# Length-39 transforms by sums and differences of q and 39 - q, as 64x64 products in quarters of the array, for the later batches of a fused filter-and-experts kernel

## The chip, the cores and the metric

The kernel runs on one core of a Trainium2 chip. The metric is the device time of one execution in microseconds (us), the median of several runs. A profile of one such execution shows every instruction of the engines: TensorE (PE for its matmuls, PEld for its weight loads), VectorE (DVE), ScalarE (ACT), GpSimd (POOL) and SyncE (SP, which here only issues DMAs). Everything is float32.

## What is computed

Two layers, one after the other, on `x` of 8 batches x 2496 tokens x 256 channels:

```python
X = np.fft.rfft(x, axis=1)                 # along the 2496 tokens
Y = X * (filt_r + 1j * filt_i)[None]
y = np.fft.irfft(Y, n=2496, axis=1)        # then (8*2496, 256)

logits = y @ w_gate                        # 8 experts
e = argmax(logits); gate = softmax(logits)[e]
out = gate * (relu(y @ w1[e]) @ w2[e])     # token by token, 256 -> 1024 -> 256
```

## The kernel before

**The transform.** 2496 = 39 x 64, and 39 and 64 have no common factor, so the long transform is a 39 x 64 transform in two dimensions. A token is named by a pair (q, t), q below 39 and t below 64. For each batch there are four stages on TensorE, each with its own table as the stationary operand:

- stage A (`stage_a`, L336): the real length-39 transform over q. Three values of t lie below each other in the partitions, so a table of 3 x 39 = 117 rows and 3 x 40 = 120 columns (`tas`) turns a tile of 117 partitions into 20 real and 20 imaginary coefficients for three t. A batch has 64 values of t in 22 columns of 256 channels. They come in chunks of four (`CH`: five chunks of four and one of two); a matmul takes two columns, 512 elements, so a full chunk costs two matmuls (L342).
- stage B (L356) and stage C (L382): the length-64 transform and its inverse, 128 x 128 tables; between them DVE multiplies by the filter (L363 to L372).
- stage D (`stage_d`, L391): the inverse length-39 transform, the same shape as A turned round: 120 rows in, 117 rows out (L401; the batch's last two columns L405, one of 120 rows and one of 40).

Between A and B and between C and D the data goes through DRAM (`zd`, `ud`), which turns it: A's result is stored with 120 partitions, B reads 64 and 64. After each matmul of A and D the function `evac` copies the PSUM bank to SBUF on DVE or ACT, whichever its own estimate (`either`) says is free first. Batch 0 takes another way (`first_a` and so on), with no DRAM.

**Routing.** Stage D's result `yo` is transposed on TensorE (`turn_y`, L476), multiplied by the gate's weights (`logits`, L490, four products of 32 columns each next to each other in the array), turned back (L501), and some 20 small DVE operations (`route`) find each token's expert and its place in a list of rows in DRAM. GpSimd then scatters the rows with one indirect DMA for each column (`scatter`, L617): 22 for a batch.

**The experts.** As soon as a batch's rows are listed, tiles of 512, 256 or 128 rows of one expert are loaded (`rows_in`), transposed (L750), multiplied by w1 (L793, seven products in place of eight by sums that GpSimd and DVE form, or L834 without them), then by w2 (L851), scaled by the gate (L856) and scattered to the output by GpSimd (L857).

**The order.** The whole program is one hand-made order: every engine's instructions are issued in the order in which a planner in the kernel's last part emits them. `slot(k)` lists the transform's steps of one round with a place in the round and a price in us of TensorE: in slot k stand stages B and C of batch k, stage A of batch k+1 and stage D and routing of batch k-1. `experts()` yields the experts' pieces, and the main loop mixes the two streams, so that TensorE has expert work between transform steps. An engine takes its instructions strictly in that order: where one waits, all behind it on the same engine wait. `now`, `free` and `lands` are the planner's estimates; nothing measures at run time. `more_loads` issues the loads of x, z and u ahead, through 7 buffers (`NIN`), in the order in which the steps will need them. After about 930 us the transform is over and only experts' work is left.

Of the kernel before, what the change touches and what calls it, by code (L numbers as in the profile page):

```python
# [38 lines left out]

def token(q, t):  # L40
    return (q * N2 * pow(N2, -1, N1) + t * N1 * pow(N1, -1, N2)) % S


def coefficients():

    k = np.arange(S)
    of = np.zeros((N2, N1), int)
    of[k * pow(N1, -1, N2) % N2, k * pow(N2, -1, N1) % N1] = k
    return of[:, :NF]


def dft_tables():
# [27 lines left out]
    for j in range(NB):  # L80
# [6 lines left out]

    return {
# [6 lines left out]
        "valid": valid.reshape(TP, NG),  # L95
    }


def lay_x(x):

    out = np.zeros((x.shape[0], P, NG, D), x.dtype)
    q = np.arange(N1)
    for j in range(NB):
        for i in range(len(range(j, N2, NB))):
            out[:, j * N1:(j + 1) * N1, i] = x[:, token(q, NB * i + j)]
    return out
# [12 lines left out]
def kernel(  # L119
# [13 lines left out]
    valid: bass.AP,  # L133
    out: bass.AP,
# [47 lines left out]
    tas = cst.tile([TP, TK], F32, name="tas")  # L182
    tbs = cst.tile([P, P], F32, name="tbs")
    tcs = cst.tile([P, P], F32, name="tcs")
    tds = cst.tile([TK, TP], F32, name="tds")
# [6 lines left out]
    tri = cst.tile([TP, TP], F32, name="tri")  # L192
    ones = cst.tile([TP, P], F32, name="ones")
    segs = {w: cst.tile([P, E * w], F32, name=f"seg{w}") for w in (8, NG % 8)}
    ids0 = cst.tile([TP, NG], F32, name="ids0")
    vld = cst.tile([TP, NG], F32, name="vld")
# [63 lines left out]
    def load_rest():  # L260
        nc.sync.dma_start(out=tds, in_=td)
        nc.vector.memset(wg, 0.0)
        nc.sync.dma_start(out=wg[:, :, :E], in_=moe_w_gate.rearrange("(i p) e -> p i e", p=P))
        nc.sync.dma_start(out=ids0, in_=ids)
        nc.sync.dma_start(out=vld, in_=valid)

    def make_constants():
# [3 lines left out]
            out=tri, in_=ones[:, :TP], compare_op=ALU.is_gt, fill=0.0, base=0, pattern=[[1, TP]], channel_multiplier=-1  # L271
# [15 lines left out]
    def columns(ap, i0, n):  # L287
# [4 lines left out]
        if m < n:  # L292
            yield NS, slice(m, n), rows[(NG - 1) * TK:, :].rearrange("(i p) d -> p i d", p=NS)

# [29 lines left out]
    def load_z(b, c):  # L324
        f0, n = FH[c]
        zi = fin(("z", b, c))
        nc.sync.dma_start(out=zi[:HP, :n], in_=zd[b][:, f0:f0 + n, :])
        nc.sync.dma_start(out=zi[HP:, :n], in_=zd[b][:, NF + f0:NF + f0 + n, :])

    def load_u(b, c):  # L330
        i0, n = CH[c]
        ui = fin(("u", b, c))
        for r, m, v in columns(ud[b], i0, n):
            nc.sync.dma_start(out=ui[:r, m], in_=v)

    def stage_a(b, c):  # L336
        i0, n = CH[c]
        xt = ins.pop(("x", b, c))
        zo = sb.tile([TK, 4, D], F32, tag="st", name="zo", bufs=4)
        for j in range(0, n, 2):  # L340
            p = bank()
            mm(p[:TK, :], lhsT=tas, rhs=xt[:TP, j:j + 2, :], start=True, stop=True)  # L342
            evac(zo[:, j:j + 2, :], p[:TK, :].rearrange("p (t d) -> p t d", t=2), 512)
# [31 lines left out]
    def stage_c(b, f):  # L375
# [8 lines left out]
        if j == 2:  # L384
            f0 = f - 2
            move(ud[b][:, f0:f0 + 4, :], uo[:HP])
            move(ud[b][:, NF + f0:NF + f0 + 4, :], uo[HP:])
# [3 lines left out]
    def stage_d(b, c):  # L391
        if c == 0:
            lgs[b] = sb.tile([TP, NG, E], F32, tag="lg", name="lg")
# [3 lines left out]
        yo = outs["o", b, c] = sb.tile([P, 4, DR], F32, tag="y", name="yo", bufs=YB)[:TP]  # L397
        for j in range(0, n, 2):
            p = bank()
            if i0 + j + 2 < NG:  # L400
                mm(p[:TP, :], lhsT=tds, rhs=ui[:TK, j:j + 2, :], start=True, stop=True)  # L401
            else:

                for i, k in enumerate((TK, NS)):
                    mm(p[:TP, i * D:(i + 1) * D], lhsT=tds[:k, :], rhs=ui[:k, j + i, :], start=True, stop=True)  # L405
# [6 lines left out]
    def first_a(c):  # L412
# [6 lines left out]
        for j in range(0, n, 2):  # L419
            p = bank()[:, :4 * TK]  # L420
            for h in range(DH):
                for i in range(2):
                    mm(p[:, (2 * h + i) * TK:(2 * h + i + 1) * TK], lhsT=xt[:TP, j + i, h * P:(h + 1) * P], rhs=tas,
# [46 lines left out]
    def turn_y(b, c):  # L470
        yo = outs["o", b, c]
        for j in range(0, CH[c][1], 2):
            pt = bank().rearrange("p (i q) -> p i q", i=4)
            for i in range(2):
                for dh in range(DH):
                    nc.tensor.transpose(  # L476
                        pt[:, 2 * i + dh, :TP], yo[:, j + i, dh * P:(dh + 1) * P], ident[:TP, :TP]
                    )
            yt = yts[b, c, j] = sb.tile([P, 4, TP], F32, tag="yt", name="yt", bufs=4)
            evac(yt, pt[:, :, :TP], 4 * TP)  # L480

    def logits(b, g):
# [4 lines left out]
        lt = psr.tile([P, 2, E * NG], F32, tag="rk", name="lt")[:, :, :TP]  # L487
# [4 lines left out]
        ls = sb.tile([P, 2, TP], F32, tag="ls", name="ls", bufs=1)  # L492
# [3 lines left out]
    def turn_logits(b):  # L496
        g, w, ls = outs.pop(("l", b))
        n = w // CT
        pt = bank()[:TP, :2 * w].rearrange("p (i w) -> p i w", i=2)
# [8 lines left out]
    def route(b, g):  # L508
        t0 = 8 * g
        w = min(8, NG - t0)  # L510
        lg = lgs[b][:, t0:t0 + w]
        sh3 = (TP, w, E)
        she = (TP, E, w)

        def small(name, *shape, dt=F32, tag=None, rows=TP):
# [12 lines left out]
        nc.vector.tensor_tensor(oh, oh, em8[:TP, None, :].to_broadcast(sh3), op=ALU.mult)  # L528
# [4 lines left out]
        nc.vector.tensor_tensor(idx, idx, vld[:, t0:t0 + w], op=ALU.mult)  # L533
# [3 lines left out]
            oe, idx[:, None, :].to_broadcast(she), em8[:TP, :, None].to_broadcast(she), op=ALU.is_equal  # L537
# [10 lines left out]
        mm(rk[:TP, 0, :E * w], lhsT=tri, rhs=oef, start=True, stop=True)  # L548
        mm(rk[:, 1, :E * w], lhsT=ones, rhs=oef, start=True, stop=True)
        rks = sb.tile([P, 2, 8 * E], F32, tag="rks", name="rks", bufs=1)  # L550
        nc.vector.tensor_copy(rks[:TP, 0, :E * w], rk[:TP, 0, :E * w])
# [5 lines left out]
        for c, yo in enumerate(yos):  # L557
            n = min(4, w - 4 * c)
            sh8 = (TP, n, 8)
            nc.vector.tensor_scalar(  # L560
                yo.bitcast(I32)[:, :n, D:D + 8], in0=ids0[:, t0 + 4 * c:t0 + 4 * c + n, None].to_broadcast(sh8),
# [13 lines left out]
        nc.vector.tensor_tensor(posf, runf[:TP], rks[:TP, 1, :E * w], op=ALU.subtract)  # L575
        nc.vector.tensor_tensor(posf, posf, rks[:TP, 0, :E * w], op=ALU.add)
        yield 2
        bs = sb.tile([TP, E], F32, tag="bs", name="bs", bufs=1)
        nc.vector.tensor_tensor(bs, cnt[:TP], eoff[:TP], op=ALU.add)
# [6 lines left out]
        row = sb.tile([TP, 8], U32, tag="row", name="row", bufs=2)[:, :w]  # L586
        nc.vector.tensor_copy(row, rowf)  # L587
# [539 lines left out]
```

## Time and profile before

| What | Value |
|---|---|
| time, median of 3 runs (lowest to highest) | 1552.96 us (1546.85 to 1555.91) |
| span of the profiled execution | 1552.7 us |
| TensorE matmuls, share of the span | 97% |
| DVE, ACT, POOL | 48%, 33%, 43% |
| DMA engines, mean share in the queue of SyncE | 52.0% |
| chain of work that ended last: TensorE's share | 78% |
| stage A of batches 4 to 7 begins / ends on TensorE | 177.0 us / 678.2 us |
| stage D of batches 3 to 7 begins / ends on TensorE | 304.3 us / 930.0 us |

A float32 matmul stands in the trace as two matmul instructions, each with its own weight load, so the trace counts 154 instructions for 77 matmuls at L342. A matmul's printed duration includes the way through the array, which overlaps with the next one; what a matmul costs a busy TensorE is read from start to start.

### The profile page before, as it was taken

Reading aid. Unit: us, or ns where it says so; the run is one execution under the profiler, and the core shown is the slowest. Engines: PE = TensorE matmul, PEld = TensorE weight load, DVE = VectorE, ACT = ScalarE, POOL = GpSimd, SP = SyncE. Lnnn points to the kernel's source line nnn. Section 1 sums busy time; section 2 is a strip of 40 time slices with the busy share of each in tenths; the row PEclk is TensorE's granted clock in tenths of the full one; section 3 lists DMA queues with packets and bytes.
Section 4 is the critical chain, followed back from the end, with each engine's and each line's share of the span. In section 5 each row is a group of like instructions: output and inputs, shape, how many; then the busy total and the mean of one; then the engine's idle time right before and its main releaser. Section 6 shows DMA issues by size and latency. Waiting matters only on the chain.

```text
span 1552.7 us, 23781 instructions
## 1 busy us (share of the span) xinstructions
PE 1500.8 (97%) x7524; PEld 1192.7 (77%) x7524; DVE 749.1 (48%) x1916; ACT 519.9 (33%) x1053; POOL 669.6 (43%) x814
## 2 busy tenths in 40 slices
PE   7997898999999999999999999999999999999998
PEld 6543454877678767788788778888888889989997
DVE  4676666434656555455755444675334334430000
ACT  3443433333333333233332333322222232224343
POOL 3322344313545444455356544573546455631111
PEclk9999999999999999999999999999999999999999
DMA  9759897785796386444844643435454436665651
GB/s 235 186 162 288 260 293 238 244 260 169 239 293 186 113 237 207 132 154 134 205 132 134 165 149 124 145 121 184 161 174 173 154 116 184 182 234 179 180 179 38
DMA packets 118465, 285.18 MB, mean 184 GB/s; under 512 B 17411, under 2 KB 58380, under 8 KB 118341
## 3 DMA queue, kind: packets, MB, share of 16 engines
q1 hardware_dynamic: 99221, 240.32, 52.0%
q0 software_dynamic: 19120, 43.33, 8.0%
q8 instruction: 63, 1.03, 0.3%
q14 instruction: 61, 0.50, 0.1%
HBM read 203.58 MB, written 80.64 MB: 183 GB/s over the span
## 4 chain that ended last, share of the span: by engine, by line
PE 78%; DMA 9%; issue 7%; DVE 4%; SPq 0%; ACT 0%; POOL 0%; POOLq 0%; DVEq 0%; ACTq 0%
PE bank L851 31%; PE bank L793 23%; PE bank L401 4%; PE bank L342 4%; PE bank L356 4%; DMA out_dram<-ys,idt 3%; PE bank L382 3%; PE bank L834 3%; PE bank L750 2%; PE bank L476 2%; DMA fin<-in_x_dram 2%; PE lt L490 1%; DMA fin<-ud 1%; DMA ud<-uo 1%; DVE hT L797 1%
## 5 line engine op out<-in xcount | busy, mean ns | idle before, releaser
L851 PE MATMUL bank<-w2t,hT 128*128 128x256 f32 x2240 | 499.1, 380 | 2.5 <-DMA w2t<-in_moe_w_dram 2.4
L851 PEld LDWEIGHTS bank<-w2t,hT 128*128 128x128 f32 x2240 | 421.0, 190 | 73.0 <-issue 13.8
L797 DVE TENSOR_TENSOR hT<-bank,hT 128x512 f32<-128x512 f32 (+1 forms) x504 | 299.6, 627 | 279.4 <-PE bank L793 189.8
L857 POOL DMA_INDIRECT out_dram<-ys,idt x161 | 159.2, 989 | 505.4 <-ACT ys L856 219.9
L617 POOL DMA_INDIRECT rows<-yo,row x176 | 174.5, 992 | 179.2 <-DVE row L587 61.8
L801 ACT ACTIVATE hT<-hT 128x1024 f32<-128x1024 f32 (+1 forms) x144 | 133.2, 957 | 319.6 <-DVE hT L797 319.6
L856 ACT ACTIVATE ys<-bank,gts 128x256 f32<-128x256 f32 x156 | 73.8, 475 | 408.2 <-PE bank L851 354.2
L793 PE MATMUL bank<-xT,w1t 128*128 128x256 f32 (+1 forms) x864 | 190.3, 356 | 0.0
L793 PEld LDWEIGHTS bank<-xT,w1t 128*128 128x128 f32 x864 | 151.6, 190 | 21.9 <-issue 4.3
L793 PE MATMUL bank<-sums,wsum 128*128 128x256 f32 (+1 forms) x576 | 135.5, 358 | 0.0
L834 PEld LDWEIGHTS bank<-xT,w1t 128*128 128x128 f32 x864 | 116.2, 193 | 15.6 <-issue 9.5
L834 PE MATMUL bank<-xT,w1t 128*128 128x128 f32 (+1 forms) x864 | 126.6, 302 | 1.5 <-DMA w1t<-in_moe_w_dram 1.5
L793 PEld LDWEIGHTS bank<-sums,wsum 128*128 128x128 f32 x576 | 100.4, 190 | 19.6 <-issue 9.6
L744 DVE COPY idt<-xg 128x4 int32<-128x4 int32 (+2 forms) x63 | 18.0, 286 | 168.5 <-DMA out_dram<-ys,idt 142.6
L768 POOL TENSOR_TENSOR wsum<-w1t 128x256 f32<-128x256 f32 x72 | 52.9, 734 | 102.7 <-PE bank L793 77.6
L363 DVE TENSOR_TENSOR ys<-bank,ht 128x512 f32<-128x512 f32 x80 | 54.9, 687 | 75.4 <-PE bank L356 74.8
L840 ACT ACTIVATE hT<-bank 128x128 f32<-128x128 f32 (+1 forms) x214 | 63.7, 301 | 56.1 <-PE bank L834 50.7
L401 PE MATMUL bank<-fin,tds 120*117 120x512 f32 x140 | 69.4, 617 | 8.5 <-DMA fin<-ud 7.4
L851 PE MATMUL bank<-w2s,hT 128*128 x336 | 76.0, 379 | 0.0
L342 PE MATMUL bank<-fin,tas 117*120 117x512 f32 x154 | 73.5, 595 | 2.4 <-DMA fin<-in_x_dram 2.0
L382 PE MATMUL bank<-ys,tcs 128*128 128x512 f32 x140 | 73.0, 603 | 3.0 <-DVE ys L372 3.0
L356 PE MATMUL bank<-fin,tbs 128*128 128x512 f32 x140 | 73.2, 606 | 1.6 <-issue 1.4
(151 smaller groups left out, 1758.9 us busy)
## 6 DMA issues: line engine op xcount, KB each, us to landing
w1t<-in_moe_w_dram SPq DMA_DIRECT2D x126, 512.0 KB
w2t<-in_moe_w_dram SPq DMA_DIRECT2D x84, 512.0 KB
fin<-in_x_dram SPq DMA_DIRECT2D x39, 512.0 KB
fin<-zd SPq DMA_DIRECT2D x70, 256.0 KB
ud<-uo SPq DMA_DIRECT2D x70, 256.0 KB
zd<-zo SPq DMA_DIRECT2D x35, 480.0 KB
fin<-ud SPq DMA_DIRECT2D x35, 480.0 KB
xg<-rows SPq DMA_DIRECT2D x28, 544.0 KB
```

The costliest lines, as they stand in the source:

```text
L342: mm(p[:TK, :], lhsT=tas, rhs=xt[:TP, j:j + 2, :], start=True, stop=True)
L356: mm(p, lhsT=tbs, rhs=zi[:, j:j + 2, :], start=True, stop=True)
L382: mm(p, lhsT=tcs, rhs=ys, start=True, stop=True)
L401: mm(p[:TP, :], lhsT=tds, rhs=ui[:TK, j:j + 2, :], start=True, stop=True)
L617: sc = nc.gpsimd.indirect_dma_start(out=rowsd, out_offset=bass.IndirectOffsetOnAxis(ap=at, axis=0), in_=what, in_offset=None,)
L793: mm(q[:, v], lhsT=left[:, v * P:(v + 1) * P], rhs=right, start=True, stop=True)
L797: nc.vector.tensor_tensor(o, q, a, op=ALU.add)
L801: nc.scalar.activation(o.rearrange("p v r c -> p v (r c)"), q.rearrange("p v r c -> p v (r c)"), AF.Relu)
L834: mm(p[:, :m], lhsT=w1t[2 * i + g][:, dh, fh, v * P:(v + 1) * P], rhs=xts[i][:, dh, :m], start=(dh == 0), stop=(dh == DH - 1))
L851: mm(p[:, :D], lhsT=hs[i][k % 4 // 2][:, k // 4, k % 2, j * P:(j + 1) * P], rhs=w2, start=(k == 0), stop=(k == FT - 1))
L856: lambda: nc.scalar.activation(ys, p[:, :D], AF.Copy, scale=gate))
L857: nc.gpsimd.indirect_dma_start(out=out, out_offset=bass.IndirectOffsetOnAxis(ap=idt[i].bitcast(U32)[:, j, :], axis=0), in_=ys, in_offset=None,
```

## The change

Stage A of batches 4 to 7 (`SUMS_A = 4`) and stage D of batches 3 to 7 (`SUMS_D = 3`) use the symmetry of the length-39 transform. With s = x[q] + x[39-q] and d = x[q] - x[39-q], the real coefficients are a 20 x 20 cosine table times s, and the imaginary ones a 20 x 20 sine table times d. With three t below each other a table has 60 rows and columns, which fits in 64, so four such products fit beside each other in the 128 x 128 array. For that:

- x of those batches is laid out by `sums_places`: rows 0-63 and 64-127 hold two groups of three t, half of a chunk's columns hold x[q] for q = 0 to 19 and the other half x[39-q].
- GpSimd forms the differences (`difference`) and DVE the sums (`total`: 2 x[q] - d), in place, in steps of their own ahead of stage A.
- Stage A does four matmuls of 64 rows and 64 columns for a full chunk in place of two of 117 and 120: two row halves, times two column halves, into two PSUM banks. DRAM's `zd` holds real and imaginary parts apart, and a store takes four DMAs of 60 partitions.
- Stage D does the same four products for each chunk, then ACT copies the sine part, and DVE adds and subtracts it (`low`, `high`), which replaces the two copies.
- `yo` has 124 rows instead of 117, some of them empty. Their rows are given a place beyond the list (`off`), and the scatter leaves out what lies beyond (`bounds_check`).
- Tables, token numbers and validity marks for the new layout are loaded over the old ones between batches (`ta2`, `td2`, `other_tables`).

```diff
+NI = 11
+TR2 = 2 * (64 - 4) + 4
+SUMS_A, SUMS_D = 4, 3
...
+    def sum_columns(ap, i0, m):
...
+        for k in range(2):
+            for r in range(2):
...
+                yield slice(at, at + n), slice(k * m, (k + 1) * m), v
...
     def load_u(b, c):
         i0, n = CH[c]
         ui = fin(("u", b, c))
+        if b >= SUMS_D:
+            for r, m, v in sum_columns(ud[b], 2 * c, n // 2):
+                nc.sync.dma_start(out=ui[r, m], in_=v)
+            return
...
+    def difference(b, c):
+        m, xt = CH[c][1] // 2, ins["x", b, c]
+        nc.gpsimd.tensor_tensor(xt[:, m:2 * m], xt[:, :m], xt[:, m:2 * m], op=ALU.subtract)
...
+    def total(b, c):
+        m, xt = CH[c][1] // 2, ins["x", b, c]
+
+        nc.vector.scalar_tensor_tensor(
+            out=xt[:, :m], in0=xt[:, :m], scalar=2.0, in1=xt[:, m:2 * m], op0=ALU.mult, op1=ALU.subtract)
...
     def stage_a(b, c):
...
+        if b >= SUMS_A:
+            m = n // 2
+            for k in range(2):
+                p = bank()[:, :m * D]
+                for g in range(2):
+                    o = 64 * (g ^ k)
+                    mm(p[o:o + 64], lhsT=tas[64 * g:64 * g + 64, 64 * k:64 * k + 64],
+                       rhs=xt[64 * g:64 * g + 64, k * m:(k + 1) * m, :], start=True, stop=True)
+                evac(zo[:, k * m:(k + 1) * m, :], p.rearrange("p (i d) -> p i d", i=m), m * D)
+            for r, at, v in sum_columns(zd[b], 2 * c, m):
+                move(v, zo[r, at])
...
     def stage_d(b, c):
...
+        if b >= SUMS_D:
+            m = n // 2
+            ps2 = [bank()[:, :m * D], bank()[:, :m * D]]
+            for k in range(2):
+                for r in range(2):
+                    g = 64 * (r ^ k)
+                    rows = 3 * NF if i0 + n < NG or r == 0 else NF
+                    mm(ps2[k][64 * r:64 * r + 64], lhsT=tds[g:g + rows, 64 * k:64 * k + 64],
+                       rhs=ui[g:g + rows, k * m:(k + 1) * m, :], start=True, stop=True)
+            pe, po = (p[:TR2].rearrange("p (i d) -> p i d", i=m) for p in ps2)
+
+            low, high = yo[:, :m, :D], yo[:, m:n, :D]
+            nc.scalar.copy(out=high, in_=po)
+            nc.vector.tensor_tensor(low, pe, high, op=ALU.add)
+            nc.vector.tensor_tensor(high, pe, high, op=ALU.subtract)
...
+            return
...
+        if b >= SUMS_D:
+            nc.vector.tensor_tensor(row, rowf, off[:, t0:t0 + w], op=ALU.add)
...
             out_offset=bass.IndirectOffsetOnAxis(ap=at, axis=0),
             in_=what,
             in_offset=None,
+            bounds_check=TR - 1,
+            oob_is_err=False,
         )
...
+                at, key = (0.25 if k == 0 else 0.0) + 0.7 * c / nch, ("x", k + 1, c)
+                if k + 1 >= SUMS_A:
+                    at += 0.1
+                    steps.append((at - 0.1, lambda c=c: difference(k + 1, c), key, 0.0))
+                    steps.append((at - 0.05, lambda c=c: total(k + 1, c), key, 0.0))
...
+        if k == SUMS_A - 2:
+            steps.append((0.85, lambda: nc.sync.dma_start(out=tas, in_=ta2), None, 0.0))
+        if k == SUMS_D + 1:
+            steps.append((0.02, lambda: nc.sync.dma_start(out=tds, in_=td2), None, 0.0))
+        if k == SUMS_D:
+            steps.append((1.99, lambda: sides.append(other_tables()), None, 0.0))
```

## The prediction

> **What bounds the kernel now.** I read the page's busy line and the chain of waits first, then the same busy times cut by stretch, then single instructions.
>
> ```profile
> PE 1500.8 (97%) x7524; PEld 1192.7 (77%) x7524; DVE 749.1 (48%) x1916; ACT 519.9 (33%) x1053; POOL 669.6 (43%) x814
> ...
> PE 78%; DMA 9%; issue 7%; DVE 4%; SPq 0%; ACT 0%; POOL 0%; POOLq 0%; DVEq 0%; ACTq 0%
> ```
>
> TensorE is busy 97% of the span and is 78% of the chain that ended last. A mean can hide a stage with another limit, so here are the stretches in which the changed stages lie (columns: stretch, its length, then busy time of PE, weight loads, DVE, ACT and POOL with their counts, clock, DMA share, GB/s):
>
> ```profile
> 175.00:255.00 80.00, 66.24 (x269) 38.40 (x264) 48.54 (x170) 28.13 (x60) 27.93 (x29) 0.94 0.84 258
> 255.00:430.00 175.00, 173.98 (x770) 128.24 (x769) 88.89 (x250) 62.67 (x133) 71.41 (x80) 0.99 0.76 238
> 430.00:610.00 180.00, 177.60 (x805) 135.32 (x805) 106.31 (x258) 61.95 (x106) 88.48 (x105) 1.00 0.69 208
> 610.00:765.00 155.00, 155.00 (x729) 121.87 (x728) 86.57 (x191) 48.78 (x85) 68.33 (x82) 1.00 0.54 157
> 765.00:930.00 165.00, 164.05 (x803) 130.92 (x802) 87.42 (x230) 53.79 (x92) 89.58 (x108) 1.00 0.49 146
> ```
>
> From 255 to 930 us TensorE lacks 4.4 us of 675: it always has work, since expert pieces fill what the transform leaves, and after 930 us only expert work follows. So a microsecond of TensorE time taken out after 255 us comes off the end, unless a new wait eats it. In 175:255 it lacks 13.8 us of 80, at a DMA share of 0.84: there DMA sets part of the pace. Stage A of batch 4 (177.0 to 234.1 us) lies in that stretch, everything else that changes lies later. Busy time counts the overlapping tails of matmuls, so the price of one is read from start to start (columns: start, length, engine, line, tiles, shape, count):
>
> ```profile
> 509.23 1.03 PE L793 MATMUL bank<-xT,w1t 128*128 128x256 f32 x4
> 510.09 1.21 PE L405 MATMUL bank<-fin,tds 120*117 120x256 f32 x4
> 511.24 1.13 PE L793 MATMUL bank<-sums,wsum 128*128 128x256 f32 x4
> ...
> 513.07 1.03 PE L793 MATMUL bank<-xT,wsum 128*128 128x256 f32 x4
> 514.02 1.01 PE L490 MATMUL lt<-yt,wg 128*32 128x234 f32 x16
> 514.96 1.09 PE L750 MATMUL bank<-ident,xg 128*128 128x128 f32 x8
> 515.89 3.62 PE L851 MATMUL bank<-w2t,hT 128*128 128x256 f32 x16
> 519.35 1.02 PE L356 MATMUL bank<-fin,tbs 128*128 128x512 f32 x2
> 520.21 3.62 PE L851 MATMUL bank<-w2t,hT 128*128 128x256 f32 x16
> 523.66 0.96 PE L476 MATMUL bank<-ident,yo 117*128 117x117 f32 x8
> 524.46 0.82 PE L851 MATMUL bank<-w2t,hT 128*128 128x256 f32 x3
> ```
>
> 16 instructions of 256 elements take 519.35 - 515.89 = 3.46 us, 0.216 each; a 512-element matmul (two instructions) takes 520.21 - 519.35 = 0.86. The line to dwell on is L490: four products of 32 columns, each with its own stream of 234 elements, 16 instructions in 514.96 - 514.02 = 0.94 us. One behind the other they would take 16 x 0.216 x 234/256 = 3.16. So float32 products beside each other in the columns run four abreast: 3.16/4 = 0.79, and 0.94 - 0.79 = 0.15 is left over. A further 0.09 lies ahead of it (513.07 + 4 x 0.216 = 513.93, start at 514.02). I put entry and exit of such a group at **0.25** together.
>
> **What the Trainium skill says.** "TensorEngine Tiling (Array Packing)", section "Tiling Modes", has it that tiles run independently and that a change of the tiling mode drains TensorE; the 0.94 us and the 0.25 us agree. "PSUM — Partial Sum Buffer", section "PSUM bank collisions raise a hardware error", says that different row tiles cannot use one PSUM bank at a time, but that the error comes for the same 32-partition quadrant. In the change two row halves write one bank, in different partition halves, at the same time. No trace of before has row halves side by side, so this cost is bounded below from both sides. "SBUF — State Buffer", section "SBUF: two separate sides", says that a GpSimd operation and a DVE operation with two SBUF inputs exclude each other for a whole instruction; the new difference and sum are such a pair, and so are L369 and L372:
>
> ```profile
> L372 DVE TENSOR_TENSOR ys<-ys,yw 128x512 f32<-128x512 f32 x67 | 51.7, 772 | 2.3
> L369 POOL TENSOR_TENSOR ys<-ys,yw 128x512 f32<-128x512 f32 x13 | 16.5, 1273 | 33.6 <-DVE yw L365 29.8 <-PE bank L342 3.1 <-PE bank L356 0.7
> ```
>
> L372's median is 693 ns and its longest 1789, which fits a wait of about one GpSimd operation.
>
> **The change part by part.**
> *Stage A, full chunk.* Before: two matmuls, 1.72 us. After: four products of 512 elements; if four abreast, two instruction rounds of 0.43 = 0.86, plus 0.25 = 1.11. Saved 0.61. If only the column halves ran abreast, 2 x 0.86 + 0.25 = 1.97, a loss of 0.25. I take the first: L490 shows four streams at once, and the four products use disjoint parts of the array. The last chunk (256 elements): 0.86 before, 0.43 + 0.25 = 0.68 after, saved 0.18. Four batches: 20 x 0.61 + 4 x 0.18 = **12.9 us**.
> *Stage D.* The same 0.61 for a full chunk. The last chunk, L405, took 511.24 - 510.09 = 1.15, so 0.47 is saved. Five batches: 25 x 0.61 + 5 x 0.47 = **17.6 us**.
> *124 rows for 117.* L476: 8 in 524.46 - 523.66 = 0.80, 0.10 each; 220 of them grow by 7/117, 1.3 us. L490: 14 more elements, 0.012 us for each of 4 rounds in 15 groups, 0.7 us. **-2.0 us**.
> TensorE in sum: 12.9 + 17.6 - 2.0 = 28.5 us less.
> *GpSimd.* 20 differences at 1.27 (L369) and 4 at about 0.7 (a 256-element row such as L756 has 667 ns): 28 us, in the some 500 us before stage A of batch 7 ends. POOL is at 41% to 49% in 255:610 and goes to about 51%. Behind a difference on GpSimd's queue wait scatters and sums of w1; TensorE waits for those only later (one wait of 1.1 us for them from 175 to 930 us).
> *DVE.* 24 sums (0.77, or 0.4) 17 us; in D 50 operations at about 0.66 (between L797's 627 and L363's 687 ns) and 10 short ones, 37 us, against copies that go away: by the order of instructions DVE's 18 copies of `yo` become 3. Some 40 us net on 369 us busy in 255:930, 55% to 61%. Stage A's first two products wait for the sum on DVE and the other two for the difference on GpSimd. The steps stand 0.05 and 0.1 of a round ahead, the planner holds stage A until its estimate of them is over, and expert pieces fill that time; if the real queues are later than the estimate, TensorE stands.
> *SyncE and DMA.* 157 more issues at about 0.45 us (L301's median is 0.47), 71 us over 755; weight loads queue behind them. SyncE spends 219 us of the span waiting for TensorE to free `w1t`, so it has room. Bytes stay the same, and 120 KB pieces of 60 partitions have the same 1 KB rows as the 480 KB ones. I cost this at nothing.
> *Scatters.* L857 has the bounds check already: 989 ns, against L617's 992 without it. Nothing. The reloads of tables wait for the last use of the old, some slots ahead of the first use of the new: nothing.
> *Waits.* Stage A of batch 4 saves 3.2 us where DMA sets part of the pace; I count half as lost, 1.6. For new waits on `difference`, `total` and the longer path to `yo` I allow 2 us.
> Sum: 28.5 - 1.6 - 2 = 25 us; 1553 - 25 = **1528 us**.
>
> **Rivals.**
> *New waits eat half.* The sum path adds two engines between a load and stage A, and DVE blocked behind GpSimd delays all PSUM copies. If each of the 24 A chunks holds TensorE for 0.55 us, 13 us go: 1541. For it: GpSimd often waits itself (scatter L617 up to 27.8 us for `row`). Against it: TensorE's waits in these stretches are tiny today, under the same kind of dependence on GpSimd.
> *They eat all of it*: 1.0 us for each of 24 differences: 1553, no change.
> *Row halves take turns* in the array or the bank: 45 full chunks lose 0.25 each, 4 short A chunks 0.24, the D short ones gain 0.05: 12 us, with the 2 us of longer rows 14: **1567, slower**. For it: the skill's sentence on row tiles and one bank. Against it: it names an error, not a pause, and the quadrants differ.
>
> **How the numbers follow.** The forecast 70%, half eaten 14%, all eaten 6%, turns 10%. Faster is the first two, 0.84; same 0.06; slower 0.10. The range leaves out the turns and the outer edges. Its low end: entry and exit cost nothing for half of the 54 groups (27 x 0.25 = 7 us) and no wait is added (4 us), 1517. Its high end is the case in which all is eaten, 1552.
>
> **What would show it.** In the changed profile, four 64 x 64 products of 512 elements take about 1.1 us from start to start up to the next line, with starts a few ns apart in each round; 2 us would mean turns. The stretches from 255 to 930 us keep TensorE above 97%, and the transform's end moves from 930 to about 905 us. A TensorE wait of 10 us or more in total on `fin` from DVE or POOL would be the first rival. The prediction is wrong if the groups cost far more than 0.25 to enter and leave, or if DVE at 61% holds up `hT` for the w1 products.

## The result and the profile after

The changed kernel takes **1570.29 us** (median of 4 runs, 1570.03 to 1572.53), the kernel before beside it 1552.34 (1546.85 to 1555.91): ratio **1.0122**, 95% interval 1.0090 to 1.0154. It is slower, and outside the range of 1517 to 1552. A second series gave 1.0117 (1.0081 to 1.0153).

The busy line and the chain of the changed kernel's page, to hold against the first two lines shown of before:

```profile
PE 1494.2 (95%) x7748; PEld 1171.2 (75%) x7748; DVE 799.9 (51%) x1978; ACT 516.0 (33%) x1055; POOL 738.9 (47%) x838
...
PE 62%; issue 8%; DVE 7%; DMA 7%; ACT 1%; SPq 1%; POOL 0%; POOLq 0%; DVEq 0%; ACTq 0%
```

TensorE is busy only 7 us less, DVE 51 us more, GpSimd 69 us more, and TensorE's share of the chain falls from 78% to 62%: the end is now reached through other engines more often. The stretches, with the same columns as before:

```profile
175.00:255.00 80.00, 65.74 (x312) 36.00 (x310) 54.61 (x183) 30.54 (x69) 35.74 (x35) 0.91 0.85 261
255.00:430.00 175.00, 159.19 (x778) 116.75 (x778) 86.56 (x230) 54.67 (x120) 76.19 (x80) 0.95 0.71 216
430.00:610.00 180.00, 172.21 (x862) 122.04 (x861) 135.44 (x303) 63.19 (x112) 112.72 (x112) 1.00 0.72 213
610.00:765.00 155.00, 150.92 (x741) 115.07 (x740) 95.00 (x209) 46.44 (x81) 77.51 (x86) 0.99 0.60 171
765.00:930.00 165.00, 165.00 (x863) 127.59 (x861) 102.25 (x261) 53.12 (x96) 94.40 (x103) 1.00 0.49 140
```

In 255:765, where TensorE had lacked 3.4 us of 510, it now lacks 27.7. What it waits for from 60 to 930 us (columns: waiting line, releaser, us in total, times, longest):

```profile
PE bank L449 <- DVE fin L434: 10.7, 4, 7.9
PE bank L449 <- DMA tas<-in_ta_dram: 8.7, 1, 8.7
PE bank L473 <- DMA fin<-zd: 6.4, 2, 5.8
PE bank L537 <- DMA fin<-ud: 5.0, 1, 5.0
PE bank L934 <- DVE hT L938: 4.5, 5, 2.3
```

Before, the longest wait on `tas`' products (L342) was 0.9 us, and `fin<-zd` was not in the list at all. (Lines of the changed kernel: A by quarters L449, D by quarters L523, difference L427, total L434, stage B L473, scatter L756, `hT` L938.)

**The quarters run four abreast, but their group costs 0.10 us more than forecast.** TensorE's timeline around one full chunk of A, up to the next one of D (columns as before):

```profile
617.48 3.62 PE L992 MATMUL bank<-w2t,hT 128*128 128x256 f32 x16
621.03 1.09 PE L449 MATMUL bank<-fin,tas 64*64 64x512 f32 x8
622.05 3.72 PE L992 MATMUL bank<-w2t,hT 128*128 128x256 f32 x16
625.70 1.09 PE L523 MATMUL bank<-fin,tds 60*64 60x512 f32 x8
```

Eight instructions take 622.05 - 621.03 = 1.02 us. The sixteen ahead take 3.55 to the next start, where sixteen took 3.46 before: 0.09 of entry. That is 1.11, the forecast's figure. But something is lost behind the group as well: sixteen instructions with a group of quarters both behind and ahead of them take 625.70 - 622.05 = 3.65, 0.10 more than the 3.55. So a full chunk costs 1.21, against 1.72 before, and saves 0.51 instead of 0.61. (In the whole trace the median is 0.093 ahead of a group and 0.104 behind it, with hardly any spread.) The row halves, two of which write one bank at the same time, do not take turns.

I then split each run's span in two: for every line and shape the median time from start to start (TensorE's own work), and all that lies above it (waits, the slow clock after them, entries and exits of groups). The time ahead of the first product and behind the last, 11.4 us in both, is left out. Work falls from 1469.9 to 1445.4 us, **24.5 less**; the rest rises from 71.4 to 112.0, **40.6 more**. The difference, 16.1, is that of the two spans (1568.8 - 1552.7). Some 10 of the 40.6 are the entries and exits of 54 groups at 0.09 and 0.10. So TensorE is relieved of only 14 us, and the question for the chip is where some 30 us of new waits come from; 17 of the 40.6 lie in 175:300.

### The profile page after: what moved, and what is told of

It is laid out like the page before. It is cut to its first block, busy times and chain, and to the rows that moved or that the text cites. A ratio compares the mean times of both kernels' runs of the same rounds, so it can differ in the third digit from the quotient of the medians.

```text
span 1568.8 us, 24828 instructions
## 1 busy us (share of the span) xinstructions
PE 1494.2 (95%) x7748; PEld 1171.2 (75%) x7748; DVE 799.9 (51%) x1978; ACT 516.0 (33%) x1055; POOL 738.9 (47%) x838
## 3 DMA queue, kind: packets, MB, share of 16 engines
q0 software_dynamic: 28080, 43.49, 9.0%
## 4 chain that ended last, share of the span: by engine, by line
PE 62%; issue 8%; DVE 7%; DMA 7%; ACT 1%; SPq 1%; POOL 0%; POOLq 0%; DVEq 0%; ACTq 0%
PE bank L992 29%; PE bank L934 21%; DMA out_dram<-ys,idt 4%; PE bank L975 2%; PE bank L523 2%; PE bank L499 2%; DVE hT L938 2%; PE bank L891 2%; PE bank L473 2%; PE bank L612 1%; DMA zd<-zo 1%; PE bank L449 1%; PE lt L626 1%; DVE yw L482 1%; DVE yw L481 1%
## 5 line engine op out<-in xcount | busy, mean ns | idle before, releaser
L992 PEld LDWEIGHTS bank<-w2t,hT 128*128 128x128 f32 x2240 | 420.4, 190 | 75.0 <-issue 10.7
L938 DVE TENSOR_TENSOR hT<-bank,hT 128x512 f32<-128x512 f32 (+1 forms) x504 | 299.9, 627 | 291.2 <-PE bank L934 206.2
L756 POOL DMA_INDIRECT rows<-yo,row x176 | 213.9, 1215 | 150.0 <-issue 81.7
L975 PEld LDWEIGHTS bank<-xT,w1t 128*128 128x128 f32 x864 | 114.4, 192 | 14.5 <-issue 3.6
L473 PE MATMUL bank<-fin,tbs 128*128 128x512 f32 x140 | 77.1, 637 | 7.9 <-DMA fin<-zd 6.4
L934 PE MATMUL bank<-xT,wsum 128*128 128x256 f32 (+1 forms) x288 | 67.9, 358 | 1.5 <-DVE hT L938 1.5
L992 PEld LDWEIGHTS bank<-w2s,hT 128*128 128x128 f32 x336 | 62.2, 190 | 7.6
```

Source lines behind the costliest of these rows:

```text
L473: mm(p, lhsT=tbs, rhs=zi[:, j:j + 2, :], start=True, stop=True)
L756: sc = nc.gpsimd.indirect_dma_start(out=rowsd, out_offset=bass.IndirectOffsetOnAxis(ap=at, axis=0), in_=what, in_offset=None, bounds_check ...
L934: mm(q[:, v], lhsT=left[:, v * P:(v + 1) * P], rhs=right, start=True, stop=True)
L938: nc.vector.tensor_tensor(o, q, a, op=ALU.add)
L975: mm(p[:, :m], lhsT=w1t[2 * i + g][:, dh, fh, v * P:(v + 1) * P], rhs=xts[i][:, dh, :m], start=(dh == 0), stop=(dh == DH - 1))
L992: mm(p[:, :D], lhsT=hs[i][k % 4 // 2][:, k // 4, k % 2, j * P:(j + 1) * P], rhs=w2, start=(k == 0), stop=(k == FT - 1))
```

## The experiments

Chips differ (before took 1551 to 1554 us in four series and 1565 and 1568 in two), so every kernel is read as a ratio to before on its own chip; 0.001 is 1.55 us. Where ratios from different chips are compared, it is taken for granted that a chip slows all kernels alike; after was not run on the slower two. The splits hold each trace against the one trace of before (span 1552.7 us), so on the slower two chips they contain some 13 and 15 us that are the chip's. "After" stands for the changed kernel.

**Each half alone.** Edits: `SUMS_A, SUMS_D = 4, 8` (A only) and `= 8, 3` (D only).

> Stage A alone by quarters (batches 4 to 7), stage D as before. Theory 1 (several separate leaks: the reload of the table tas, the queue through GpSimd and VectorE ahead of stage A, and the last chunk of D): TensorE's own work falls by about 13 us, the waits of the changed trace in front of stage A (8.7 us for tas, 10.7 us for the sum) come back almost whole, so 1556 to 1562. Rival (stage D is the culprit: slower scatters of 124 rows, copy, add, subtract): 1540 to 1545.

> Stage D alone by quarters (batches 3 to 7), stage A as before. Theory 1: 17.6 us less expected on TensorE, minus 8 us for the last chunks (2.29 us each instead of 0.68), minus 2 us for longer rows, and a few us of waits behind VectorE and behind scatters of 1.32 us: 1548 to 1556. Rival (stage A's sum path is the whole loss): 1543 to 1546. Rival (stage D is the culprit): 1565 or more.

A only: 1573.25 us, ratio 1.0133 (1.0103 to 1.0162). D only: 1568.21, ratio 1.0089 (1.0059 to 1.0119). Both times lie outside theory 1, D's alone in the range of the rival "stage D is the culprit": each half alone loses about as much as both together. By the split, A only has 15.0 us less work and 33.2 more of the rest, 18 of them in 175:300; D only 9.3 less and 24.4 more, 17 of them in 765:930. So the loss has no single seat, and the two do not add: both together have 40.6, not 58.

**The last chunk of D.** In the batch's last chunk two of the four products have 60 rows and two have 20, in turn. TensorE's timeline of after:

```profile
390.27 2.36 PE L523 MATMUL bank<-fin,tds 60*64 60x256 f32 x8
392.55 1.04 PE L626 MATMUL lt<-yt,wg 128*32 128x248 f32 x16
```

2.28 us here, 2.29 in the median of the five, for a chunk forecast at 0.68. Taken one by one, the eight instructions start one behind the other, 0.27 and 0.31 us apart. The edit gives every product 60 rows (the missing 40 are filled with any data; their table rows are zero):

```diff
+                if r.stop - r.start == NF:
+                    fill = ud[b].rearrange("t s d -> (t s) d")[:2 * NF, None, :]
+                    nc.sync.dma_start(out=ui[r.stop:r.stop + 2 * NF, m], in_=fill)
...
-                    rows = 3 * NF if i0 + n < NG or r == 0 else NF
+                    rows = 3 * NF
```

> The changed kernel, but in the last chunk of stage D all four products have 60 rows (the 40 rows without use are filled with other rows of ud by one more DMA; their results are empty rows). Theory 1: the group takes 0.6 us instead of 2.29, five times, so 8 us less than the changed kernel: 1562. Rival (TensorE's time is given back as waits, because GpSimd and VectorE pace the transform): within 3 us of the changed kernel, 1567 to 1571.

```profile
390.00 0.66 PE L526 MATMUL bank<-fin,tds 60*64 60x256 f32 x8
390.60 1.04 PE L629 MATMUL lt<-yt,wg 128*32 128x248 f32 x16
```

0.59 us now (median), four instructions starting within 0.02 us: five times 1.69, 8.5 us less work. The Trainium skill, "TensorEngine Tiling (Array Packing)", section "Tiling Modes", lists tilings by rows: 64 and 32 are different modes. 20 rows fit the smaller one, which agrees with the eight instructions of this group running no longer abreast; that they run in the smaller mode is inferred, not seen. The time fell to 1566.85, ratio 1.0089 (1.0058 to 1.0120), 3.3 thousandths or about 5 us below after, a difference no larger than the intervals. By the split, 4 of the 8.5 us come back as waits, a first sign.

**The table's reload.** TensorE in front of A's first group, and SyncE's issue of the load for it:

```profile
188.32 2.10 PE L449 MATMUL bank<-fin,tas 64*64 64x512 f32 x8 [8.66 <-DMA tas<-in_ta_dram]
...
180.25 0.58 SPq L1039 DMA_DIRECT2D tas<-in_ta_dram  x1
```

The old table's last product began at 157.5, but the reload stood in SyncE's queue until 180.25 and landed 8 us later. TensorE, idle for 8.66 us, then ran the group in 190.34 - 188.32 = 2.02 us instead of 1.02. Edit: `tas2`, a tile of its own, loaded at the start.

> The changed kernel, but the second table of stage A has a tile of its own, loaded at the start, so that nothing waits for the reload. Theory 1: the wait of 8.7 us in front of batch 4's first stage A goes, with the cold clock after it, 8 to 10 us less: 1560 to 1562. Rival (the wait moves on to the next late load or to the sum, as that stretch is paced by DMA): at most 3 us less, 1567 or more.

1568.67 us, ratio 1.0119 (1.0079 to 1.0159). The wait on the table is gone, the time is not: the rival was right. In 175:255 the excess falls from 7.2 to 2.3, in 300:430 it grows from 3.1 to 7.0 (and falls from 7.8 to 5.7 in 430:520). The next late input stands behind the first.

**The scatters.** GpSimd's scatter group in after, and then in the kernel with `TR2 = P`, 128 rows instead of 124 (columns: count, then busy us and mean ns):

```profile
L756 POOL DMA_INDIRECT rows<-yo,row x176 | 213.9, 1215 | 150.0 <-issue 81.7
...
L756 POOL DMA_INDIRECT rows<-yo,row x176 | 176.0, 1000 | 159.7 <-issue 83.3 <-DVE cnt L727 24.4 <-ACT lg L278 20.1
```

> The changed kernel with 128 rows instead of 124 in yo and all routing tiles (four more empty rows). If the row count is what makes a scatter take 1.32 us, it falls to 0.99 and GpSimd gets 110 x 0.33 = 36 us back; if the rows beyond the list make it slow, it stays at 1.32. Theory 2 (GpSimd's one queue carries scatters, differences and w1 sums, and its lateness reaches TensorE): 5 to 10 us less than the changed kernel, 1560 to 1565. Rival (scatters wait for data anyway and hold nobody): within 2 us, 1568 to 1571.

The median of a 124-row scatter is 1.32 us, that of the 117-row ones with the same bounds check 0.99 and of the 128-row ones 0.98. So it is the number of rows and not the check: 110 scatters x 0.33 = 36 us of GpSimd's 69. The packets of the software queue rise with it: 28080 in after, 19120 before, 17520 with 128 rows. 1572.34 us against 1565.11 on this chip, ratio 1.0045 (1.0025 to 1.0065): of all single repairs the one that gives most, some 12 us by the ratios, with TensorE's work up by 1.2.

**The three repairs together** (last chunk, 128 rows, and the reload moved up: `steps.append((0.59, ...tas...))` for 0.85).

> Three repairs together: 60 rows in every product of stage D's last chunk, the reload of tas issued right behind the last stage A that uses the old one, and 128 rows. Theory 1 (separate leaks add up): 4 + 2 + 5 us less than the changed kernel, 1558 to 1561. Rival (what one repair frees the next wait takes, since another engine paces the transform): 1565 to 1568.

1564.36 against 1565.11, **ratio 0.9995** (0.9981 to 1.0008). The whole loss is back, but no gain: TensorE's work is now 31.7 us below before, and the rest 43.7 above, some 13 of which are the chip's.

**Taking the added work off again.** Without the steps `difference` and `total` (A's products take x as it is loaded), and with two plain copies in place of D's copy, sum and difference; the numbers differ in both. A's steps keep the place 0.1 of a round later that they have in the change.

```diff
-                    steps.append((at - 0.1, lambda c=c: difference(k + 1, c), key, 0.0))
-                    steps.append((at - 0.05, lambda c=c: total(k + 1, c), key, 0.0))
```

```diff
-            nc.scalar.copy(out=high, in_=po)
-            nc.vector.tensor_tensor(low, pe, high, op=ALU.add)
-            nc.vector.tensor_tensor(high, pe, high, op=ALU.subtract)
+            evac(high, po, m * D)
+            evac(low, pe, m * D)
```

> As e7_mend3, with GpSimd's differences and VectorE's sums left out (stage A then works on x[q] and x[39-q] as they are, so the numbers are others). If the sum path in front of stage A is the main source of the new waits: 12 to 16 us less than e7_mend3, 1545 to 1548. If stage D's copy, add and subtract is: within 3 us of e7_mend3.

> As e7_mend3, with stage D's copy, add and subtract replaced by two plain copies out of PSUM on VectorE or ScalarE, as before the change (the numbers are others). If stage D's chain of three on VectorE is the main source of the new waits: 10 us or more less than e7_mend3, about 1550. If the sum path of stage A is: within 3 us of e7_mend3.

Without D's sums: ratio 0.9970 (0.9950 to 0.9989), 4 us better than the repairs alone. Without A's: **1.0134** (1.0105 to 1.0164), a plain miss. The waits of 175:300 did go (14.6 us of excess became 0.8), but a new one of 12.5 us on `fin<-zd` stands from 486.8 to 499.3, and 430:520 has 18.6 more than before (5.8 with the repairs alone). So without the sums TensorE no longer stands in 175:300, and yet the time did not fall. Leaving two steps out gives another order of everything behind them; as no engine has more to do than with the repairs alone, the 20 us are put down to that order.

**The difference on VectorE** instead of GpSimd (`nc.vector.tensor_tensor`), added to the repairs. This asks about the wait of 7.93 us at 272.6 us in after, ahead of which GpSimd had this to do:

```profile
268.43 0.98 POOL L756 DMA_INDIRECT rows<-yo,row  x1 [0.30 <-issue]
269.43 2.49 POOL L427 TENSOR_TENSOR fin<-fin 128x512 f32<-128x512 f32 x2
```

Six scatters from 261.95 on stood in GpSimd's queue ahead of two differences, and TensorE stood behind those.

> The changed kernel with its three repairs (last D chunk of 60 rows throughout, table loaded earlier, scatters of 128 rows) and the difference x[q]-x[39-q] on VectorE instead of GpSimd. Theory, that late predecessors of TensorE's in-order groups give the time back and that GpSimd's scatters in front of the differences are one of them: the wait of 7.4 us at 263 us goes, and the time is 4 to 8 us below that of the repairs alone, ratio 0.995 to 0.998 (the repairs alone had 0.9995). Rival, that VectorE is as late there, or that the wait only moves to the next input in line (loads of fin): within 2 us of the repairs alone, ratio 0.998 to 1.001.

1560.85 against 1551.97, ratio 1.0048 (1.0029 to 1.0066): worse than the repairs alone. The wait shrank, but 255:300 kept 5.1 us of excess and 765:930 has 19 more than before, where TensorE's longest wait is 3.8 us for `yo` from VectorE. The difference is cheaper there (673 ns against 1197), and it does not help.

**Quarters in A for batches 6 and 7 only** (`SUMS_A, SUMS_D = 6, 3`, with the repairs).

> The repaired kernel with stage A by quarters from batch 6 on alone (4 and 5 stay with the full products), D from batch 3 on. Theory, that quarters pay only where TensorE has expert work to put into the gaps: about 7.5 us of TensorE's work is given up, but the waits of 175 to 300 us (about 17 us more than before the change) go too: ratio 0.993 to 0.997. Rival, that waits follow the work taken out wherever it is taken out: ratio 1.000 to 1.005, above the repaired kernel with both.

Ratio 1.0003 (0.9992 to 1.0014). In the profiled execution, the fastest of the 20 (1544.9 us), the waits of 175:300 are gone (-4.4 us against before), but 520:610 has 9.0 and 690:765 has 6.9 more. The rival was right on the time: where work is taken out, waits follow.

**Does TensorE's time come off the end at all?** The kernel before, with half of one product left out of each full chunk of the same batches: 256 columns, read twice by the copy. Nothing else is added, and the order stays. The first run:

> The kernel before, its order and prices as they are; of every full chunk of stage A from batch 4 on (36) and of stage D from batch 3 on (45) the second product has 256 columns instead of 512, and its copy reads them twice, so half of that product is left out and the numbers differ. By the row of 0.86 us for a product TensorE's work falls by 81 x 0.43 = 34.8 us, and nothing is added on any engine or queue. If TensorE's time is what the end waits for, 28 to 35 us come off (ratio 0.978 to 0.982). If the order of work and the other engines' pace hold the end, as the change's loss suggests, less than half does: ratio 0.989 to 1.000. The first would say that the change lost by the work that it added to other engines, the second that the time taken off could never have reached the end in this order.

Its count was wrong: there are 20 chunks in A and 25 in D, so 45 x 0.426 = 19.2 us. And the changed numbers sent tokens to other experts: two blocks of experts more, 14.5 us of TensorE. It measured 1.0003 (0.9990 to 1.0016) and tells little until that is taken off. The second run halves D's first product instead, which leaves the experts' work as before:

```diff
-                mm(p[:TK, :], lhsT=tas, rhs=xt[:TP, j:j + 2, :], start=True, stop=True)
-                evac(zo[:, j:j + 2, :], p[:TK, :].rearrange("p (t d) -> p t d", t=2), 512)
+                mm(p[:TK, :D], lhsT=tas, rhs=xt[:TP, j, :], start=True, stop=True)
+                evac(zo[:, j:j + 2, :], p[:TK, None, :D].to_broadcast((TK, 2, D)), 512)
```

> The kernel before with half of one product left out of every full chunk of stage A from batch 4 on (20 chunks, second product) and of stage D from batch 3 on (25 chunks, first product): 256 columns, which the copy reads twice; order and prices as before, numbers differ. There are 45 such chunks, not the 81 told for the run before it, and its halves were chosen so that the experts should get as many blocks as before (its forerunner had two blocks more, 14.5 us of TensorE). TensorE's work falls by 45 x 0.43 = 19.2 us. If TensorE's time comes off the end: 14 to 19 us less, ratio 0.988 to 0.991. If the order holds the end: ratio 0.996 to 1.001. A block of experts more or fewer is worth 7.2 us and is to be taken out of the comparison.

1537.92 against 1551.48: **ratio 0.9921** (0.9891 to 0.9951), 13.6 us for 19.2. The page counts the same 161 scatters of results as before. By the split of the two traces, work fell by 19.0 us and the rest rose by 3.5 only. So the first step of the prediction stands: TensorE's time comes off the end, at some 70% (40% to 88% by the interval).

**And the added work alone?** The kernel before with its full products, plus A's difference on GpSimd and a second difference on VectorE that brings x back, 0.1 of a round ahead of A as in the change, and D's copies by fixed engines with one more pass of VectorE.

```diff
+                if k + 1 >= 4:
+                    at += 0.1
+                    steps.append((at - 0.1, lambda c=c: difference(k + 1, c), key, 0.0))
+                    steps.append((at - 0.05, lambda c=c: total(k + 1, c), key, 0.0))
...
+            elif j == 0:
+                nc.vector.tensor_copy(o, pv)
+            else:
+                nc.scalar.copy(out=o, in_=pv)
+                nc.vector.tensor_tensor(o, o, o, op=ALU.max)
```

> The kernel before with its full products, and with only the work that the change adds on other engines in front of and behind them: from batch 4 on the difference on GpSimd, and on VectorE a second difference that brings the old value back, before stage A (A's steps 0.1 of a slot later, as in the change); from batch 3 on D's banks copied by fixed engines, with one more pass of VectorE over half of the tile. TensorE's work is that of before. Theory, that the added work in front of TensorE's groups is what takes the time back: 10 to 25 us slower, ratio 1.006 to 1.016. Rival, that it lies beside TensorE as the prediction had it, and the loss is peculiar to the quarters: within 4 us, ratio 0.998 to 1.002.

1594.81 us, **ratio 1.0281** (1.0260 to 1.0303): 43 us slower, nearly twice the most that was expected, with the same work on TensorE to 0.1 us. But this kernel adds more than was meant. `more_loads` of the kernel before issues one load for every step that names a chunk of x. In the change a chunk has three such steps and repeats are taken out of the list; here they are not, so every chunk of x of batches 4 to 7 is loaded three times. The issues of those loads, before and then in this kernel:

```profile
fin<-in_x_dram SPq DMA_DIRECT2D x39, 512.0 KB
...
fin<-in_x_dram SPq DMA_DIRECT2D x79, 512.0 KB
```

With those of 256 KB (18 for 10) that is 48 loads more, and 308.27 MB are moved in all for 285.18. Two stretches, before and then this kernel:

```profile
175.00:255.00 80.00, 66.24 (x269) 38.40 (x264) 48.54 (x170) 28.13 (x60) 27.93 (x29) 0.94 0.84 258
255.00:300.00 45.00, 44.98 (x189) 35.09 (x188) 23.82 (x63) 15.37 (x32) 23.34 (x26) 0.95 0.87 282
...
175.00:255.00 80.00, 60.44 (x227) 34.30 (x221) 43.18 (x144) 24.32 (x53) 31.64 (x30) 0.85 0.92 292
255.00:300.00 45.00, 30.24 (x122) 18.22 (x118) 25.55 (x54) 10.96 (x21) 19.46 (x22) 0.85 0.89 287
```

TensorE loses 20.5 us of 125 there, and the clock falls from 0.94 to 0.85. Its largest wait, and what GpSimd's difference itself (L338) waited for:

```profile
PE bank L355 <- DVE fin L344: 21.8, 6, 8.0
...
  DMA fin<-in_x_dram: 27.0, 4
```

GpSimd stands for 27.0 us until x has landed, at a DMA share of 0.92. Then come a difference (1.3 us), a total (0.7), and only then TensorE, where before TensorE took x as it landed. The path is the change's own: in after, with x loaded once, GpSimd's differences stand 26.2 us in eight waits for x. But how much of the 43 us is the added work, and how much the 48 added loads, this kernel can't tell, so it doesn't show what the added work costs alone.

**Both at once**, the shorter products and the added work (with the same added loads):

> Both of the two at once: 19.2 us less on TensorE and the added work on the others, so the change's shape without quarters, without 124 rows, without a second table. If the two simply add: the sum of the two differences (say -16 + 15, ratio about 1.000). If the shorter products only lengthen the waits for the added work: as slow as the added work alone, ratio 1.005 to 1.015. If the shorter products give the added work no trouble: as fast as the less work alone.

1585.07, ratio 1.0210 (1.0183 to 1.0236), 33.6 us slower. The sum of the two would be -13.6 + 43.3 = 29.7, within the width of the intervals: they add. Beside the added work the shorter products still take 9.7 us off (1594.81 - 1585.07).

**The price.** The repaired kernel with the planner's old price of A and D, 0.43 us a column for 0.28.

> The changed kernel with the three repairs, and the planner's price of a chunk of A and D left at 0.43 us a column as before, instead of 0.28: the same instructions, another order. If the plan built from the lower prices puts too little between a load and its use, the higher price gives it room: 3 to 8 us less than the repairs alone, ratio 0.994 to 0.998. If the order isn't at fault: 0.998 to 1.001, as the repairs alone (0.9995).

1575.32, ratio 1.0142 (1.0119 to 1.0166), a miss: 23 us slower than the repairs alone by the ratios of two chips, with the same instructions in another order. The low price is the better one; what it says of the kernel is how much the order alone is worth.

**An eighth buffer for loads, and late batches only.** `NIN, YB = 8, 5` with the repairs; and `SUMS_A, SUMS_D = 6, 5` with the repairs.

> The repaired kernel with 8 buffers for loads instead of 7, and 5 for y instead of 6 (the room is from there). Theory, that x arrives too late for load, difference, total, product: the waits on the total and on fin at 175 to 300 us shrink by half, 6 to 10 us less than the repairs alone, ratio 0.993 to 0.997. Rival, that GpSimd's and VectorE's own queues make the total late, or that a buffer less for y costs as much: ratio 0.998 to 1.004.

> The repaired kernel with A by quarters from batch 6 on and D from batch 5 on. TensorE's work falls by 7.5 us in A and by 3/5 of D's 20.1, 12 us, together 19.5. Theory, that it is kept where expert work stands between a late input and TensorE: 5 to 14 us less than before, ratio 0.991 to 0.997. Rival, that the added work takes the gain away in late batches too: 0.998 to 1.003.

1645.64 against 1567.61, ratio 1.0505 (1.0483 to 1.0527), and 1578.62, ratio 1.0075 (1.0050 to 1.0101). Both missed. The first tells nothing of the loads: two things were changed, and the rest rises in every stretch from 60 to 930 us, by 118 us in all. The second has 17.5 us less work and 47.2 more of the rest, spread over 300 to 850 us: late batches don't keep the gain either. (Some 15 us of the 118 and the 47.2 are the chip's.)

The unaltered changed kernel went along with the difference on VectorE, A from batch 6 and the first shorter products:

> The changed kernel once more, unaltered, so that the three that run with it on the same chip can be held against it. Ratio to the kernel before 1.012 as the first time; 1.009 to 1.015 would be no surprise.

It is the 1.0117 given at the top.

## Why the prediction was wrong, step by step

- **TensorE bounds the kernel, and its time comes off the end:** right, and now shown by the shorter products, at 0.71 us for each us. Where the rest is lost wasn't followed up.
- **A full chunk at 1.11 us, four abreast:** four abreast is right; entry and exit of 0.25 is too small, as 0.10 behind each group is missing. (The prediction took its 0.25 from L490 and what lies ahead of it; in its own lines L750 behind L490 takes 0.93, elsewhere 0.88.) A chunk costs 1.21. A's work fell by 15.0 us, less 24 groups at 0.20: 10.3 for 12.9. The rival with turns came near the time (1567) by a mechanism that did not occur.
- **D, 17.6 us: mis-sized.** 48.6 fell to 36.9, less 30 groups at 0.20: 5.8. The failed term is the last chunk at 0.68, where 20 rows beside 60 took 2.29 and the entry and exit. With 60 rows throughout it would be 14.3.
- **124 rows, -2.0:** 2.3. TensorE in sum: 14 us less, where 28.5 was forecast.
- **Scatters, nothing: failed.** The row shown for it had 128 rows; 124 take a third longer, 36 us of GpSimd. Repairing this gave about 12 us.
- **Reloads of tables, nothing: failed.** The old table was free in time, but the reload's place in SyncE's queue was late: 8.7 us of waiting. Mending it alone gave no measurable gain.
- **New waits, 3.6 us: the step on which the forecast fell.** It took "TensorE's waits in these stretches are tiny today" for room. They were some 30 us. Those that the trace names stand largely in 175:300: 8.7 us for the table, 7.9 for a total that had waited for GpSimd and the scatters in its queue, 5.8 for a load of z. The named rival, waits on `fin` from DVE of 10 us or more in total, occurred (10.7). The rival "they eat all of it" came near the sum of the waits (24 and the 3.6), by luck: they are not 1.0 us at each difference, and they met a saving half as large as forecast, so the kernel came out slower and not even.
- **Counting busy time of GpSimd and DVE:** the sums were nearly right (GpSimd 28.6 us for differences, as forecast; GpSimd at 53% in 255:610 for 51%, DVE at 62% in 255:930 for 61%), and beside the point. Neither engine is full; TensorE stood for the moment at which one operation was done, as at 272.6.

The balance: -24.5 us of work, some 10 of entries and exits, some 30 of waits. Against the forecast of 25 us less, some 15 us are saving on TensorE that did not come, and some 26 are waits.

**What stays open.** Why some 30 us of waits arose is shown only in part: the scatters' rows account for some 12 us, and the waits of 175:300 go when the sums are left out. The kernel with the added work also loaded x three times and moved A's steps, so what the added work costs alone isn't separated, and the kernel before with A's steps moved and nothing else wasn't run. Orders of the same instructions differ by 23 us here (the price), and leaving steps out can cost 20, so a time of one edit always contains a new order. Whether a plan made by measured landing times would keep the 21 us of the repaired kernel (31.7 less 54 entries and exits) wasn't tried. No version here beats the kernel before by more than its interval, apart from two that leave part of the computation out.

## What to carry to other kernels

When an engine is busy all the time under an order fixed beforehand, a cheaper operation on it is worth its time only if its inputs get no later: price the way from the load to the operation (who has to touch the data in between, and what stands ahead in their queues), not only their busy share. One kernel settles whether the time comes off at all: one that only takes it off. Its counterpart, one that only adds the work, is worth as much, but its loads and bytes have to be held against those of before, or it tests something else too, as it did here. When a group divides the array in another way, look at the instruction behind it too, not only at the group. And ask for every odd size (20 rows beside 60, 124 rows of 128) whether a trace shows that very size.

## What the runs showed of the hardware

- A group of 64 x 64 float32 products side by side, two of them writing one PSUM bank from different row halves, takes 1.02 us for four of 512 elements, plus 0.09 ahead of it and 0.10 behind. Two with 20 rows beside two with 60 make a group of half the length take 2.29 instead of 0.59.
- An indirect store of 124 partitions takes 1.32 us, of 117 0.99, of 128 0.98 (medians).
- After 8.66 us of idling TensorE's next group took twice its time (2.02 for 1.02), with a granted clock of 0.50 in that stretch; after 7.93 us another took 2.03, also at 0.50.
- The Trainium skill, "SBUF — State Buffer", section "SBUF: two separate sides", has GpSimd and a DVE operation with two SBUF inputs exclude each other. The total, median 684 ns, took up to 1739 in after, about one difference (1.2 us) longer. All six totals above 0.9 us ran beside an elementwise operation of GpSimd; beside scatters alone none took over 0.69. With the difference on VectorE too, its mean fell from 783 to 662 ns.
